# Attention and SwiGLU on one core: V loads behind a cast, wider dummies, block 10 one output later, loads held from chunk 20

## The chip, the cores and the metric

The kernel runs on one core of a Trainium2 chip. The metric is the device time of one execution in microseconds. Each kernel is run several times, and the median of the runs is compared. One more execution is recorded by the hardware profiler; all lines of the profile come from it.

The engines are called PE (matmuls; PEld is its weight load), DVE (vector), ACT (scalar), POOL (GpSimd) and SP (sync). In this kernel POOL issues the loads, SP issues transposing DMAs, and ACT issues the output DMAs. DMAs that POOL issues convert from 32 bits to 16 as they go.

## The reference

q, k and v have 8 batches, 8 heads, 576 positions and 64 features. Causal attention with a window of 64 is followed by a SwiGLU block over 4608 tokens of 512 features:

```
scores = where((0 <= i - j) & (i - j < 64), q @ k.T / 8, -1e9)
x = (softmax(scores) @ v), heads side by side            # 4608 x 512
out = (silu(x @ w_gate) * (x @ w_val)) @ w_out           # 512 -> 1536 -> 512, 32-bit result
```

## The kernel before, in words

**Tiles.** Tokens are cut into 36 chunks of 128; four chunks make one of 9 token groups of 512. For a chunk n, the scores (`S`, lines 454 to 518) are small matmuls of kT and qT; ACT takes the exponential into pt, DVE multiplies with a mask (`m`, line 526). `AV` multiplies pt with v, DVE divides by the sums into xb, and x is transposed into xT, by PE (`X`, line 723) or by a DMA of SP (line 714). From chunk 8 on two chunks are handled together: `P` (lines 1003 to 1014) is the first half of AV for n and n+1, the scores of n+2 and n+3, and the second half. `F` c.f (line 767) is one of 12 column blocks of gate and value for group c: 4 + 4 matmuls of 512 columns, a tanh on ACT and two operations on DVE. `O` c.u (line 804) is the output of 128 tokens: 12 matmuls, an eviction on ACT (line 825) and the output DMA (line 828). `F` of group c needs xT of its four chunks, `O` of group c needs all its `F`.

**Order.** PE's order is written by hand. `build` writes the front: dummy matmuls (`warm`, line 754), the transposes of the first k and q, scores and AV of chunks 0 to 3, the first F of group 0. Then the list `EARLY` (line 180) follows, and from group 3 on `program` (line 1039) gives a regular order: F, F, O, P, F, m. In front of each entry `pump` (line 921) puts out what is ready of two lists: `LOADS` (line 186), which POOL issues, and `SHIPS` (line 194), the transposes that SP issues (Tk14 and Tq14 are those of chunk 14, x8 that of xb of chunk 8). Both are strictly in order. An entry like `k14@O0.1` waits, in its list, until O0.1 is in the program, and carries a semaphore wait for the end of the first PE operation of that entry; on POOL, everything listed behind it waits too. k and q of chunks 0 to 7 come in pairs (k2.2 are chunks 4 and 5) and are transposed on PE (`T2`, line 404).

**Front loads.** `loads` (line 861) puts out, in this order: k of chunks 0 and 1 by SP and ACT (`first_loads`, line 730); q of chunks 0, 1 and k, q of chunks 2, 3 by POOL; constants by DVE and POOL (masks, lines 317 to 335); then on POOL v of chunks 0 to 3, gate and value weights (`load_w`; `W(0, 2)` is both for column blocks 0 and 1), and `shift`: copies of half of a v chunk into the buffer vs, which AV of chunks 1 to 3 reads. `first_T` (line 736) begins with a cast of the loaded k on DVE (line 739; in the profile under line 295) and goes on with the first transposes of PE.

**Waits.** `_Graph.emit` puts a semaphore wait in front of an instruction for each dependence that its engine has not seen yet. `op(..., after=x)` adds one on x. PSUM banks are chosen by a planner's estimate of when they are free.

Of the kernel before, what the change touches and what calls it, by code (L numbers as in the profile page):

```python
# [166 lines left out]
class _Kernel:  # L167
# [12 lines left out]
    EARLY = """  # L180
        V F0.4 F0.5 F0.6 k2t q2t F0.7 S4 F0.8 H4.1.1/act H5.0.1/act B4 F0.9 X4/act+ k3t A5 N5 F0.10 X5/act+ q3t F0.11 S6
        F1.0-1a F1.2-3a B6 F1.4-5a F1.6-7a X6/act+ A7 N7 F1.8-9a X7/act F1.10-11a F1.0-1b F1.2-3b S8 S9 F1.4-5b F1.6-7b
        O0.0 F1.8-9b O0.1 P8 m10 m11 F1.10-11b O0.2 P10 O0.3 X10/act X11/act m12 O1.0 m13 F2.0 F2.1 F2.2 F2.3 F2.4 O1.1
        P12 F2.5 m14 F2.6 m15 F2.7 O1.2 P14 F2.8 m16 F2.9 m17 F2.10 F2.11 O1.3 K O2.0
    """
    LOADS = """
        k2.2 q2.2 Wg8-10 Wv8-10 v4 v5 Wg10-12 Wv10-12 k3.2 q3.2 v6 v7 k8 q8 k9 q9 Wo0-6 k10 q10 k11 q11 Wo6-12 v8 h6.1.0
        h7.0.0 v9 k12 q12 k13 q13 v10 v11 k14@O0.1 q14 k15 q15 v12 v13 k16 q16 k17 q17 v14 k18 q18 v15 k19 q19 q20 v16
        k20 q21 v17 k21 q22 v18 v19 k22@F3.4 q23@F3.4 k23@F3.4 q24@F3.4 v20@F3.4 k24@O2.3 q25@O2.3 v21@F3.4 k25@O2.3
        q26@O2.3 v22@O2.3 k26@O3.1 q27@O3.1 v23@O2.3 k27@O3.1 q28@O3.1 v24@O3.1 k28@O3.3 q29@O3.3 v25@O3.1 k29@O3.3  # L190
        q30@O3.3 v26@O3.3 k30@O4.1 q31@O4.1 v27@O3.3 k31@O4.1 q32@O4.1 v28@O4.1 k32@O4.3 q33@O4.3 v29@O4.1 k33@O4.3
        q34@O4.3 v30@O4.3 k34@O5.1 q35@O5.1 v31@O4.3 k35@O5.1 v32@O5.1 v33@O5.1 v34@O5.3 v35@O5.3
    """
    SHIPS = """
        Tk8 Tq8 Tk9 Tq9 Tk10 Tq10 Tk11 Tq11 Tk12 Tq12 Tk13 Tq13 x8 x9 Tk14 Tq14 Tk15 Tq15 Tk16 Tq16 Tk17 Tq17 x12 x13
# [206 lines left out]
    def T2(self, st, x, engs):  # L402
        g = self.g
        src = (self.ks2 if x == "k" else self.qs2)[st % 2]
        dst = self.kT if x == "k" else self.qT
        z0 = (2 * st) % self.NZ
        for cc in range(2):
            bank, bk = self.bank("a")
            tb = bank[:, 0:256].bitcast(BF).rearrange("p (c j t) -> p c j t", c=2, j=2)

            def pe(e, cc=cc, tb=tb):
                for c in range(2):
                    for j in range(2):
                        for p in range(2):
                            r = e.transpose(tb[64 * p:64 * p + 64, c, j, :], src[:, 4 * cc + 2 * c + p, j, :], self.ident[:, :])  # L415
                return r

            g.op("pe", pe, reads=["ident", ("s2", x, st % 2, 0), ("s2", x, st % 2, 1)], writes=[bk])
            d = dst[:, 2 * cc:2 * cc + 2, 128 * z0:128 * z0 + 256].rearrange("p c (t j) -> p c t j", j=2)
            a = tb.rearrange("p c j t -> p c t j")  # L420
            self.copy(engs[cc], d, a, [bk], [(x + "T", z, cc) for z in (z0, z0 + 1)])
            self.drop([(bank, bk)])
# [282 lines left out]
    def X(self, n, eng="sp", kind="f", half=False):  # L705
        if n >= NCH:
            return
        g = self.g
        ix, it, u = n % 4, (n // 4) % self.NX, n % 4
        xb = self.xb[ix]  # L710
        xo = self.xT[it][:, :, 128 * u:128 * u + 128]
        xk = [("xb", ix, 0), ("xb", ix, 1)]
        if eng == "sp":
            g.op("sp", lambda e: e.dma_start_transpose(xo, xb[:, :]), reads=xk, writes=[("xT", it, u)], dma=True)
            return
        bank, bk = self.bank(kind)
        tb = bank[:, 0:256].bitcast(BF).rearrange("p (c t) -> p c t", c=4)

        def pe(e):
            for c in range(4):  # L720
                for p in range(2 if half else 1):
                    w = 64 if half else 128
                    r = e.transpose(tb[w * p:w * p + w, c, :], xb[:, 128 * c + w * p:128 * c + w * p + w], self.ident[:, :])  # L723
            return r

        g.op("pe", pe, reads=["ident"] + xk, writes=[bk])
        self.copy(eng, xo, tb, [bk], [("xT", it, u)])
        self.drop([(bank, bk)])
# [132 lines left out]
    def loads(self):  # L861
        self.first_loads()
        self.load2(0, "q")
        self.load2(1, "k")
        self.load2(1, "q")
        self.init()
        self.init_ident()
        self.init_mask()
        self.init_nmask()
        for n in range(4):  # L870
            self.load(n, "v")
        self.W(0, 2)
        self.load_w("g", 2, 4)
        self.shift(0, 1, "pool")
        self.shift(1, 1, "pool")
        self.load_w("v", 2, 4)
        self.shift(2, 1, "pool")
        self.shift(3, 0, "pool")
        self.W(4, 6)
        self.W(6, 8)  # L880

# [157 lines left out]
    def program(self):  # L1039
        yield from self.EARLY.split()  # L1040
        for c in range(3, NFC):
            for u in range(4):
                n = 4 * c + u + 4
                yield "F%d.%d" % (c, 3 * u)
                yield "F%d.%d" % (c, 3 * u + 1)
                if c > 3 and (n < NCH or u < 3):
                    yield "O%d.%d" % (c - 1, u)
                elif c == 3 and u != 1:
                    yield "O2.%d" % max(u, 1)
                if n < NCH and u % 2 == 0:  # L1050
                    yield "P%d" % n
                yield "F%d.%d" % (c, 3 * u + 2)
                if n < NCH - 2:
                    yield "m%d" % (n + 2)
                if n >= NCH and u == 3:
                    yield "O%d.%d" % (c - 1, u)
        for u in range(4):
            yield "O%d.%d" % (NFC - 1, u)

    def build(self):  # L1060
        F, S, AV, X, T2, O = self.F, self.S, self.AV, self.X, self.T2, self.O
        self.loads()
        self.banks("a", [4, 5, 6, 7, 0, 1, 2, 3, 4, 5, 0, 1, 2, 3, 4, 5, 6, 7, 0, 1, 2, 3, 4, 5, 6, 7, 6, 7])
        self.warm(48, n=121)
        self.first_T(("dve", "act"))
        s0 = self.Sa(0)
        T2(0, "q", ("act", "dve"))
        self.Sbias(s0)
        self.warm(2)
        self.Sb(s0)  # L1070
        s1 = self.Sa(1, True)
        self.Sb(s1)
        T2(1, "k", ("dve", "act"))
        T2(1, "q", ("dve", "act"))
        self.start()
        s2, s3 = self.Sa(2), self.Sa(3)
        a0, a1, a2, a3 = self.AVa(0), self.AVa(1), self.AVa(2), self.AVa(3)
        self.AVs(a0)
        self.shift(1, 0, "dve")
        self.AVn(a0)  # L1080
        self.shift(2, 0, "dve")
        self.Sbias(s2)
        self.Sb(s2)
        self.AVs(a1)
        self.AVn(a1)
        self.Sbias(s3)
        self.Sb(s3)
        X(0, "dve", "a")
        X(1, "dve", "a")
        self.warm(1, j=2)  # L1090
        self.AVs(a2)
        self.AVn(a2)
        self.AVs(a3)
        self.AVn(a3)
        F(0, (0, 1), 0, 256)
        X(2, "act", "a")
        X(3, "act", "a")
        F(0, (2, 3), 0, 256)
        F(0, (0, 1), 256, 512)
        for n in range(4):  # L1100
            self.did |= {w % n for w in ("s%d", "a%d", "x%d", "Tk%d", "Tq%d")}
        self.main("F0.2-3b")
        self.free = set(range(8))
        self.g.now = dict.fromkeys(self.g.now, max(self.g.now.values()))
        for t in self.program():
            self.pump()
            first = len(self.g.ops)
            self.main(t)
            self.at[t] = next((o for o in self.g.ops[first:] if o.eng == "pe"), None)
        self.pump()  # L1110
        assert not any(self.queues)
        self.g.emit()
# [42 lines left out]
```

## Time and profile before

| | |
|---|---|
| median of 3 runs | 334.22 us (326.64, 334.22, 337.95) |
| profiled execution, its own time | 330.86 us |
| its span, first to last instruction | 329.1 us |
| mean granted clock of PE | 0.995 |
| PE busy | 318.7 us, 97% |
| DVE, ACT, POOL busy | 203.0, 135.8, 108.5 us |
| DMA | 39.85 MB; queue 0 (POOL's loads) 78.4%, queue 1 (transposes) 24.7% of 16 engines |
| landing of v and k loads, median | 6.2 and 5.2 us after issue |
| landing of transposes of k, median (least, most) | 5.7 us (2.5, 10.5) |

Places in the span: the first dummy starts at 1.29 us, the cast at 6.27, the first V load at 5.38, the first F at 17.76. P8 is at about 73, P10 at 78.5, P12 at 97, P14 at 106, F3.0 at 119.4, P16 at 126. From about 130 us on the order repeats every 16.8 us. POOL issues loads until 48.6 us, waits 24.47 us, issues from 73.11 to 97.7, and waits again 34.45 us.

How to read it: a line of the timeline gives start and duration in us, engine, line, operation, result<-inputs, and in brackets the idle time of the engine before it with what ended it. "issue" stands where the profile shows nothing that was waited for. A chain of waits follows the last instruction back to what released it. Landing times of DMAs and the times of single DMA packets are records of the same trace.

### The profile page before, as it was taken

To read this page: it belongs to the slowest core of one execution; us is meant where nothing else is said; L and a number is where in the kernel's file an instruction comes from. 1 tells how busy PE (TensorE), PEld (TensorE's weight loads), DVE (VectorE), ACT (ScalarE), POOL (GpSimd) and SP (SyncE) were. 2 spreads that over 40 slices of the span, in tenths; PEclk is the share of its full clock that TensorE was granted. 3 is DMA by queue.
4 is the path that set the end of the run, shared out by engine and by line. 5 is a ranking of instruction groups with operands and counts; after the bars stand their busy time and mean duration, and the time that the engine had idled before them with its cause. 6 is when DMAs were issued, how large, how long until landed. Compare 5 with 4: busy or idle time off the path is not lost.

```text
span 329.1 us, 8018 instructions
## 1 busy us (share of the span) xinstructions
PE 318.7 (97%) x3415; PEld 171.7 (52%) x3451; DVE 203.0 (62%) x351; ACT 135.8 (41%) x243; POOL 108.5 (33%) x138
## 2 busy tenths in 40 slices
PE   7799999999999999999999999999999999999997
PEld 7475568866455444454545454545454544444443
DVE  4568778738357835866666656565656566555520
ACT  2643865526434544252525252525343432332222
POOL 8899990019960000506060606060512000000000
PEclk9979999999999999999999999999999999999999
DMA  9999999999999999979999999999997111100012
GB/s 144 178 169 181 171 171 138 151 179 140 175 161 152 149 140 166 97 113 117 137 118 124 124 138 112 146 113 131 121 138 94 50 50 48 50 32 33 34 57 102
DMA packets 161571, 39.85 MB, mean 121 GB/s; under 512 B 148608, under 2 KB 157056, under 8 KB 161536
## 3 DMA queue, kind: packets, MB, share of 16 engines
q0 software_dynamic: 111056, 18.62, 78.4%
q1 hardware_dynamic: 45024, 11.22, 24.7%
q10 hardware_dynamic: 5456, 9.51, 9.9%
q8 instruction: 27, 0.44, 0.6%
q14 instruction: 8, 0.07, 0.1%
HBM read 37.75 MB, written 9.44 MB: 143 GB/s over the span
## 4 chain that ended last, share of the span: by engine, by line
PE 92%; issue 2%; DMA 2%; ACT 1%; POOL 1%; DVE 1%; POOLq 0%
PE ps L787 56%; PE ps L818 27%; PE ps L641 3%; DMA va<-in_v_dram 2%; PE ps L505 1%; PE ps L468 1%; PE ps L723 1%; PE ps L843 1%; ACT pt L480 1%; PE ps L592 1%; POOL qs L375 1%; PE ps L472 1%; PE ps L415 0%; PE ps L509 0%; ACT kT L293 0%
## 5 line engine op out<-in xcount | busy, mean ns | idle before, releaser
L795 DVE SCALAR_TENSOR_TENSOR uu<-sig,ps 128x512 bf16<-128x512 bf16 x108 | 73.8, 684 | 63.9 <-ACT sig L793 63.8
L787 PE MATMUL ps<-xT,Wv 128*128 128x512 bf16 (+1 forms) x486 | 111.1, 353 | 0.5
L787 PE MATMUL ps<-xT,Wg 128*128 128x512 bf16 (+1 forms) x479 | 108.8, 353 | 2.6 <-issue 2.4
L793 ACT ACTIVATE sig<-ps 128x512 bf16<-128x512 f32 x108 | 65.0, 602 | 77.2 <-PE ps L787 77.1
L818 PE MATMUL ps<-Wo,hT 128*128 128x512 bf16 x413 | 94.9, 379 | 0.5 <-issue 0.2
L797 DVE SCALAR_TENSOR_TENSOR hT<-uu,ps 128x512 bf16<-128x512 bf16 x108 | 74.1, 686 | 3.9 <-PE ps L787 0.2
L787 PEld LDWEIGHTS ps<-xT,Wv 128*128 128x128 bf16 x496 | 48.9, 99 | 45.3
L366 POOL DMA_DIRECT2D kn<-in_k_dram x31 | 27.9, 902 | 127.9 <-PE ps L818 93.5
L787 PEld LDWEIGHTS ps<-xT,Wg 128*128 128x128 bf16 x496 | 46.7, 98 | 42.8 <-DMA xT<-xb 0.5
L818 PEld LDWEIGHTS ps<-Wo,hT 128*128 128x128 bf16 x420 | 41.0, 98 | 48.5
L825 ACT ACTIVATE ost<-ps 128x512 f32<-128x512 f32 x35 | 20.9, 597 | 90.2 <-PE ps L818 90.2
L366 POOL DMA_DIRECT2D va<-in_v_dram x40 | 35.5, 907 | 12.6 <-PE ps L818 11.9
L366 POOL DMA_DIRECT2D qn<-in_q_dram x31 | 28.1, 915 | 0.0
L668 DVE RECIPROCAL rp<-ps 128x14 f32<-128x14 f32 (+1 forms) x28 | 5.7, 202 | 34.2 <-PE ps L641 34.2
L480 ACT ACTIVATE pt<-ps 128x512 bf16<-128x512 f32 x36 | 18.9, 599 | 7.2 <-PE ps L472 6.4
L517 ACT ACTIVATE pt<-ps 128x512 bf16<-128x512 f32 x36 | 18.6, 603 | 3.7 <-PE ps L509 3.7
L670 DVE TENSOR_TENSOR xb<-ps,rp 128x896 bf16<-128x896 f32 (+1 forms) x28 | 19.4, 692 | 1.0
L641 PEld LDWEIGHTS ps<-va,pt 64*64 64x64 bf16 x888 | 10.9, 107 | 6.1 <-issue 5.1
L641 PE MATMUL ps<-va,pt 64*64 64x65 bf16 x888 | 13.5, 194 | 0.1
L526 DVE TENSOR_TENSOR pt<-pt,kmask 128x1024 bf16<-128x1024 bf16 x18 | 12.3, 684 | 0.0
L526 DVE TENSOR_TENSOR pt<-pt,mask 128x1024 bf16<-128x1024 bf16 x14 | 9.4, 685 | 0.9 <-ACT pt L480 0.9
L472 PE MATMUL ps<-qT,kT 64*64 64x64 bf16 x288 | 7.7, 194 | 1.4 <-issue 1.4
(65 smaller groups left out, 139.8 us busy)
## 6 DMA issues: line engine op xcount, KB each, us to landing
out_dram<-ost ACTq DMA_DIRECT2D x35, 256.0 KB, 2.9
va<-in_v_dram POOLq DMA_DIRECT2D x32, 128.0 KB, 6.2
kn<-in_k_dram POOLq DMA_DIRECT2D x25, 128.0 KB, 5.2
qn<-in_q_dram POOLq DMA_DIRECT2D x25, 128.0 KB, 5.5
Wg<-in_moe_w_gate_dram POOLq DMA_DIRECT2D x6, 256.0 KB, 7.7
Wv<-in_moe_w_val_dram POOLq DMA_DIRECT2D x6, 256.0 KB, 7.7
Wo<-in_moe_w_out_dram POOLq DMA_DIRECT2D x2, 768.0 KB, 19.1
qs<-in_q_dram POOLq DMA_DIRECT2D x3, 256.0 KB, 7.3
```

The source lines that it names most:

```text
L366: self.g.op("pool", lambda e, d=d, a=a: e.dma_start(d, a), writes=ks, dma=True, after=self.hold)
L480: g.op("act", lambda e, po=po, p=p: e.activation(po, sv[p], ACTF.Exp, scale=SCALE), reads=[bx[p][1]], writes=[pk[p]])
L517: g.op("act", lambda e, po=po, p=p: e.activation(po, sv[p], ACTF.Exp, scale=SCALE), reads=[bx[p][1]], writes=[pk[p]])
L526: self.g.op("dve", lambda e: e.tensor_tensor(pt, pt, m, ALU.mult), reads=pk + [key], writes=pk)
L641: z = e.matmul(self.psa[64 * c:64 * c + 64, o:o + 65], pt[p][rows, h, 64 * a:64 * a + 64], va[m][rows, h, 0:65], start=first, stop=phase = ...
L670: g.op("dve", lambda e, d=d, num=num, rb=rb: e.tensor_tensor(d, num, rb, ALU.mult), reads=bk + [("rp", k)], writes=xk, cost=(1.0, 0.25)[k])
L787: r = e.matmul(bank[:, a * n:a * n + n], W[:, kk, f * 128:f * 128 + 128], xT[:, kk, lo:hi], start=(kk == 0), stop=(kk == NK - 1))
L793: g.op("act", lambda e, G=bank: e.activation(sig[:, 0:w], G[:, 0:w], ACTF.Tanh, scale=0.5), reads=[bk], writes=[("sig", i)])
L795: g.op("dve", lambda e: e.scalar_tensor_tensor(uu[:, 0:w], sig[:, 0:w], 1.0, G[:, 0:w], ALU.add, ALU.mult), reads=[("sig", i), gk], writes ...
L797: g.op("dve", lambda e: e.scalar_tensor_tensor(out, v3(uu), 0.5, v3(V), ALU.mult, ALU.mult), reads=[("uu", i), vk], writes=[("hT", ih, f) ...
L818: r = e.matmul(OB[:, :], hT[:, f, 128 * u:128 * u + 128], self.Wo[:, f, :], start=(f == 0), stop=(f == NF - 1), skip_group_check=mid is no ...
L825: g.op("act", lambda e: e.activation(ost[:, :], OB[:, :], ACTF.Copy), reads=[ok], writes=[("ost", io)])
```

## The change

- `loads` ends after the constants. The rest moves into `next_loads`, which `build` calls after `first_T`. The V load of chunk 0 gets a wait for the first DVE operation of `first_T`, the cast; the others stand behind it on POOL.
- Among these the order changes: shift(0, 1) goes from POOL to DVE, behind AVs of chunk 0; shift(1, 1) now stands before the gate weights of blocks 2 and 3, and the value weights of blocks 2 and 3 behind shift(3, 0).
- The dummies are 11 of 512 columns in place of 48 of 121.
- In `EARLY`, P10 comes after O0.3 (it was before it), O1.0 comes before the transposes X10, X11, and O1.1 before F2.0 (it was after F2.4). O2.1 comes before F3.0 (it was after F3.1, out of `program`).
- In `LOADS`, k14 waits for O0.2 and not O0.1; k20, q21, k21, q22, v18, v19, which had no wait of their own, wait for F2.9, and v17 comes ahead of them.

```diff
-        O0.0 F1.8-9b O0.1 P8 m10 m11 F1.10-11b O0.2 P10 O0.3 X10/act X11/act m12 O1.0 m13 F2.0 F2.1 F2.2 F2.3 F2.4 O1.1
-        P12 F2.5 m14 F2.6 m15 F2.7 O1.2 P14 F2.8 m16 F2.9 m17 F2.10 F2.11 O1.3 K O2.0
+        O0.0 F1.8-9b O0.1 P8 m10 m11 F1.10-11b O0.2 O0.3 P10 O1.0 X10/act X11/act m12 O1.1 m13 F2.0 F2.1 F2.2 F2.3 F2.4
+        P12 F2.5 m14 F2.6 m15 F2.7 O1.2 P14 F2.8 m16 F2.9 m17 F2.10 F2.11 O1.3 K O2.0 O2.1
...
-        h7.0.0 v9 k12 q12 k13 q13 v10 v11 k14@O0.1 q14 k15 q15 v12 v13 k16 q16 k17 q17 v14 k18 q18 v15 k19 q19 q20 v16
-        k20 q21 v17 k21 q22 v18 v19 k22@F3.4 q23@F3.4 k23@F3.4 q24@F3.4 v20@F3.4 k24@O2.3 q25@O2.3 v21@F3.4 k25@O2.3
+        h7.0.0 v9 k12 q12 k13 q13 v10 v11 k14@O0.2 q14 k15 q15 v12 v13 k16 q16 k17 q17 v14 k18 q18 v15 k19 q19 q20 v16
+        v17 k20@F2.9 q21@F2.9 k21@F2.9 q22@F2.9 v18@F2.9 k22@F3.4 q23@F3.4 v19@F2.9 k23@F3.4 q24@F3.4 v20@F3.4 k24@O2.3
...
         self.init_nmask()
+
+    def next_loads(self, after):
+        self.hold = after
         for n in range(4):
             self.load(n, "v")
+            self.hold = None
         self.W(0, 2)
+        self.shift(1, 1, "pool")
         self.load_w("g", 2, 4)
-        self.shift(0, 1, "pool")
-        self.shift(1, 1, "pool")
-        self.load_w("v", 2, 4)
         self.shift(2, 1, "pool")
         self.shift(3, 0, "pool")
+        self.load_w("v", 2, 4)
...
-                elif c == 3 and u != 1:
-                    yield "O2.%d" % max(u, 1)
+                elif c == 3 and u > 1:
+                    yield "O2.%d" % u
...
-        self.warm(48, n=121)
+        self.warm(11)
+        first = len(self.g.ops)
         self.first_T(("dve", "act"))
+        self.next_loads(next(o for o in self.g.ops[first:] if o.eng == "dve"))
...
         self.AVs(a0)
+        self.shift(0, 1, "dve")
         self.shift(1, 0, "dve")
```

More of the change, by code (lines that the diff above doesn't have):

```diff
@@ L187 @@
         k2.2 q2.2 Wg8-10 Wv8-10 v4 v5 Wg10-12 Wv10-12 k3.2 q3.2 v6 v7 k8 q8 k9 q9 Wo0-6 k10 q10 k11 q11 Wo6-12 v8 h6.1.0
-        h7.0.0 v9 k12 q12 k13 q13 v10 v11 k14@O0.1 q14 k15 q15 v12 v13 k16 q16 k17 q17 v14 k18 q18 v15 k19 q19 q20 v16
-        k20 q21 v17 k21 q22 v18 v19 k22@F3.4 q23@F3.4 k23@F3.4 q24@F3.4 v20@F3.4 k24@O2.3 q25@O2.3 v21@F3.4 k25@O2.3
-        q26@O2.3 v22@O2.3 k26@O3.1 q27@O3.1 v23@O2.3 k27@O3.1 q28@O3.1 v24@O3.1 k28@O3.3 q29@O3.3 v25@O3.1 k29@O3.3
-        q30@O3.3 v26@O3.3 k30@O4.1 q31@O4.1 v27@O3.3 k31@O4.1 q32@O4.1 v28@O4.1 k32@O4.3 q33@O4.3 v29@O4.1 k33@O4.3
-        q34@O4.3 v30@O4.3 k34@O5.1 q35@O5.1 v31@O4.3 k35@O5.1 v32@O5.1 v33@O5.1 v34@O5.3 v35@O5.3
+        h7.0.0 v9 k12 q12 k13 q13 v10 v11 k14@O0.2 q14 k15 q15 v12 v13 k16 q16 k17 q17 v14 k18 q18 v15 k19 q19 q20 v16
+        v17 k20@F2.9 q21@F2.9 k21@F2.9 q22@F2.9 v18@F2.9 k22@F3.4 q23@F3.4 v19@F2.9 k23@F3.4 q24@F3.4 v20@F3.4 k24@O2.3
+        q25@O2.3 v21@F3.4 k25@O2.3 q26@O2.3 v22@O2.3 k26@O3.1 q27@O3.1 v23@O2.3 k27@O3.1 q28@O3.1 v24@O3.1 k28@O3.3
+        q29@O3.3 v25@O3.1 k29@O3.3 q30@O3.3 v26@O3.3 k30@O4.1 q31@O4.1 v27@O3.3 k31@O4.1 q32@O4.1 v28@O4.1 k32@O4.3
+        q33@O4.3 v29@O4.1 k33@O4.3 q34@O4.3 v30@O4.3 k34@O5.1 q35@O5.1 v31@O4.3 k35@O5.1 v32@O5.1 v33@O5.1 v34@O5.3
+        v35@O5.3
     """
```

## The prediction, on record before the result

> **What bounds the kernel now.** I read the slices of the page first, then the chain of waits, then the waits of PE, and last the timelines of the two stretches that the change edits.
>
> ```profile
> PE   7799999999999999999999999999999999999997
> PEclk9979999999999999999999999999999999999999
> DMA  9999999999999999979999999999997111100012
> ...
> q0 software_dynamic: 111056, 18.62, 78.4%
> ...
> q8 instruction: 27, 0.44, 0.6%
> ```
> PE is full from the third slice on, so only waits of PE move the end. The DMA engines are full until 255 us: whatever PE waits for late comes through them.
>
> ```profile
> 14.19 1.43 issue
> 15.62 0.22 PE ps L472 x2
> ```
> ```profile
> 17.00:18.00 1.00, 0.96 (x30) 0.72 (x23) 0.90 (x3) 0.16 (x1) 1.00 (x2) 0.65 1.27 166
> 18.00:19.00 1.00, 1.00 (x6) 0.71 (x5) 0.95 (x3) 0.00 (x0) 1.00 (x3) 0.50 1.15 140
> ```
> These are the chain of waits from 10 to 20 us, and the table by microsecond (the third number from the right is the granted clock). In the middle of the scores of chunk 3 PE stands 1.41 us with nothing to wait for, and from 17.30 to 20.71 us the clock is 0.5, which costs half of 3.41 us, 1.7 us.
>
> ```profile
> 126.28 0.43 issue
> ```
> ```profile
> 52.03 0.83 PE L787 MATMUL ps<-xT,Wg 128*128 128x256 bf16 x6 [0.19 <-issue]
> ```
> ```profile
> PEld ps L787 <- DMA xT<-xb: 0.5, 1, 0.5
> ```
> The first is the chain of waits at block 16: by the landing records the transpose of q chunk 20 came at 126.62, so this is a DMA wait. The second is a page of instructions (below). The third is F3.0: the transpose of x15 landed at 119.34 and F3.0 began at 119.39; about 0.2 us of it is PE's. All gaps of PE together are 8.0 us.
>
> **How I read the 1.41 us.** Queue q8 carries 27 packets of 16 KB, and PE has 3415 + 3451 instructions and some 90 waits: 256 instructions a packet. PE stopped after 448 instructions of the program; with 64 ahead of the program that is 512, the end of the second packet. On this count the third packet was asked for when PE passed 256 (9.26 us), was served at 13.34, took 0.97 and PE went on at 15.62: 6.4 us. Checked at another place: PE passes 1280 at 45.08, the packet is served at 48.47, and PE, at 1536, starts again at 52.03, the 0.19 us line above. In the full stretches the packet begins 4.94, 4.77 and 4.70 us after the crossing (84.31, 97.35, 106.18 us); with 0.95 of transfer and 1.3 until PE runs, 7.0 us.
> [...]
>
> **The change, part by part.**
> Dummies. 48 narrow ones started 4.81/48 = 0.100 us apart; eleven of 512 columns are 11 x 512/121 x 0.100 = 4.7 us. They end some 0.2 us earlier, and PE then waits for the cast (6.27 to 6.94) as before: 0. But 37 dummies with their weight loads are 74 instructions fewer, so every packet border falls 74 instructions later. I moved each border by 74 in the trace. Border 512 falls in AVs of chunk 2, asked for at 10.52; with 6.4 us it comes at 16.9. Without the old stall PE would be there at about 15.7; it waits 1.2, and F0 starts at 17.8 against 17.76: 0. The border that now passes harmlessly stands at 2816 + 74, inside P12: asked for at 92.3, with 7.0 us there at 99.35, reached at 97.68: **+1.67**. The 0.19 at 52.03 goes, since 47.01 to 54.10 is 7.1 us against 6.6 to 6.9: **-0.19**.
>
> V loads. POOL issued them from 5.38 (0.9 each); behind the cast it is 7.05, 1.67 later. Behind them on POOL stand the W loads and the shifts. Wv 2-4 moves from 12.95 to about 16.05, since shift(3,0) ahead of it waits for V3 (15.36). What hides this is the queue itself: q of chunks 2, 3 lands at 10.54 and V0 at 11.37, V1 12.21; a load on an idle queue needs 2.7 us (132.15 to 134.83), so V0 from 7.05 is ready before its turn. Wv 2-4 issued at 16.05 lands by the row of 15.97 (5.6 us) at 21.6; its matmul starts at 22.26. I take 0; if the cover is gone it is +1.67, and it could be below nothing by what the thinner queue gives to the packet (C). shift(0,1) costs DVE 0.28 to 0.57 in its queue before AVn(0); X0 waits for xb1, 14.69 then 15.0, inside the wait for the packet: 0. POOL loses 0.61.
>
> Block 10 one output later. O0.3 (2.59) now stands before P10, O1.0 and O1.1 around X10, X11. Nothing is added; P10 had no wait (78.5), F2.0 started without one (85.55) and x9 landed at 84.59, so 0; F2.0 gains 2.59 of cover. P12 stays where it was. O2.1 goes ahead of F3.0, which gives x15 2.59 more: **-0.2**.
>
> k14 after O0.2. POOL waits until O0.2 ends (78.55) and not O0.1 (72.80): 5.75 later, and all loads up to v17 stand behind it, and SP's transposes behind those.
>
> ```profile
> 73.11 0.88 POOL L366 DMA_DIRECT2D kn<-in_k_dram  x1 [24.47 <-PE ps L818]
> 73.97 0.88 POOL L366 DMA_DIRECT2D qn<-in_q_dram  x1
> ```
> ```profile
> 75.64 2.55 SPq L714 DMA_TRANSPOSE xT<-xb  x2
> 78.24 1.37 SPq L399 DMA_TRANSPOSE kT<-kn  x1
> 79.65 2.37 SPq L399 DMA_TRANSPOSE qT<-qn  x1
> ```
> The first is POOL's timeline, the second SP's. x8, x9 (75.64) now run ahead of the loads (2.5 us as at 143.41, not 6.7 and 7.7), and leave the crowd. In it transposes land about 2.3 us apart, and 1.0 us alone; two fewer give back 2.0 to 3. So q15's transpose, 93.62 before, comes at 93.62 + 5.75 - 2.3 = 97.1, wanted by the scores of 15 at 97.4: 0. q17's, 105.08, comes at 108.5, wanted at 106.5: 2.0 us, of which the 1.67 in P12 already gives 1.67: **+0.3**. Bounds: -0 (crowd half as deep) and +4.3 (nothing given back).
>
> Loads from chunk 20 behind F2.9 (110.0). k20 left POOL at 89.2 but landed only at 113.12, behind the others; from 110 it lands at about 117, and the transposes of chunks 20 to 22 (until 130.4 now) are wanted by P18 at 140. Queued behind k20 on POOL are q21 to v19 and the loads @F3.4: 10 us of cover, 0. While they are held, the transposes up to q20 meet fewer packets, and PE is 2 us later at P16: **-0.43**.
>
> Sum: 1.67 - 0.19 - 0.2 + 0.3 - 0.43 = +1.15, say 1.2 us. On the profiled execution (330.86: span 329.1 and 1.8 around it) this is 332.0. The four executions known are 326.64, 330.86, 334.22, 337.95, mean 332.4; on the mean it is 333.6, on the median 335.4. I take 332.8, between the first two: +1.2 on a base of 331.6.
>
> **The clock.** A wait of 1.67 us around P12 could bring a second half-clock stretch: 1.7 us, as after 14.21. [...]
>
> **Rivals.**
> A, the forecast: small terms that nearly cancel, 332.8. Chance 0.5.
> B, slower: the held loads. If the crowd gives nothing back, q17's transpose lands at 105.08 + 5.75 = 110.83 and P14 waits 4.3; q20's at 132.4 against 130.6 adds 1.8; less 0.4 for the gaps that go: 331.6 + 5.7 = 337.3, with one more half-clock stretch 339. It decides from the moment q17's transpose lands after 106.5 plus whatever P12 waited. For it: 1.4 us of slack only. Against: x8, x9 leave the crowd. 0.2.
> C, faster: the packets come in time and the front closes up. Without stall and half clock F0 starts at 16.5, is then bound by W (Wv 2-4 at 20.3) and reaches F0.4 at 24.65 and not 26.84: -2.2; with -0.8 for the other gaps: 331.6 - 3.0 = 328.6. For it: fewer loads are queued when the packet is asked for. Against: all measured crossings in full stretches took over 3 us. [...] 0.2.
> D: the V cover is gone, +1.67 on A: 334.5. 0.1. That the V hold and the hold of k20 change nothing is within A: both loads wait in a full queue anyhow.
>
> **Numbers.** 332.8. The range takes in C less the spread of the runs and B with its clock: 327 to 339. 2% (6.7 us, about what a measurement of this kernel can tell from no change, given its spread of 11 us) is 327.5 and 340.9 on the median: faster 0.15 (C, with a base at the low runs), slower 0.1 (half of B), same 0.75.
>
> **What would show it.** POOL's first V load at 7.05 and V0 still landing near 11.4; PE's idle time inside AVs of chunk 2 and not in the scores of chunk 3; an idle stretch of 1 to 2 us inside P12 or ahead of the second scores of P14; no wait at F3.0 and P16; k14 leaving POOL 5.75 us later relative to P8. I am wrong if the front shifts by over 2 us either way, or if P12 and P14 together wait over 4 us.

## The result, and the profile after

The changed kernel takes 333.51 us in the median of 6 runs (330.36 to 334.40); the kernel before 331.38 us (326.64 to 337.95, 6 runs, the three known before among them). The ratio is 1.014 [1.010, 1.018]; in a second session, with 12 runs of the changed kernel, it was 1.008 [1.004, 1.012]. All ratios here compare fast runs alone: runs more than 1.5% above the fastest of their kernel are left out. The change makes the kernel slower by about 1%, which is less than the 2% that I took as the least that one measurement can tell; I had forecast +1.2 us on a base of 331.6, so 332.8. The profiled execution takes 333.54 us, its span 331.8.

The 40 slices and the queue of POOL's loads, from the page of the changed kernel:

```profile
PE   6789998999989899999999999999999999999997
...
PEclk9999999999999999999999999999999999999999
DMA  9999999999999993999999898989896211100012
...
q0 software_dynamic: 111056, 18.62, 76.0%
```
The front looks better than before (clock full from the first slice on), but PE has dips at slices 3, 7, 12 and 14: 17 to 25, 50 to 58, 91 to 100 and 108 to 116 us. The waits of PE in the changed kernel (in all, times, longest):

```profile
PE ps L593 <- issue: 1.6, 1, 1.6
...
PE ps L469 <- DMA qT<-qn: 1.3, 1, 1.3
PE ps L788 <- DMA Wv<-in_moe_w_val_dram: 1.2, 1, 1.2
PE ps L724 <- DVE xb L612: 1.2, 1, 1.2
PE ps L469 <- issue: 1.0, 1, 1.0
```
Line numbers are one to six higher than in the kernel before. In order of time: X0 waits for xb of chunk 0 (14.51), F0 for the value weights of blocks 2 and 3 (Wv 2-4 below; 20.13), the AV of chunk 7 has nothing to wait for (53.07, first line), the second scores of P12 wait for the transpose of q15 (98.03), those of P14 for that of q17 (108.56, last line; its transpose landed at 109.51). All gaps of PE add up to 13.1 us, against 8.0.

The same places of both profiled executions, by the operation that follows (us):

| place | before | after | difference |
|---|---|---|---|
| tanh of F0.0 | 19.69 | 17.97 | -1.71 |
| tanh of F0.2, behind the wait for Wv | 24.20 | 23.32 | -0.89 |
| tanh of F1.4-5a, the third of F1 | 50.78 | 49.89 | -0.89 |
| tanh of F1.8-9a, the fifth of F1, behind the wait at 53.07 | 55.34 | 55.86 | +0.52 |
| division in P8 | 73.84 | 74.37 | +0.53 |
| division in P12 | 98.10 | 100.07 | +1.98 |
| division in P14 | 107.20 | 110.44 | +3.24 |
| division in P16 | 127.47 | 129.88 | +2.41 |
| division in P18 | 141.61 | 144.21 | +2.60 |

So the front gains 1.7, and then loses it and 2.6 more, in four steps: F0, the wait at 53 us, P12, P14. P16, which had a wait before, gives 0.8 back. From P18 on the difference stays within 0.1.

The gain: the table by microsecond of the changed kernel, with the granted clock third from the right, where it was 0.5 before, and no wait in the scores of chunk 3.

```profile
17.00:18.00 1.00, 1.00 (x11) 0.89 (x10) 0.96 (x3) 0.03 (x1) 1.00 (x2) 1.00 1.17 146
```
Where it goes first: the chain of waits of the changed kernel, 7 to 26 us (start, duration, what).

```profile
7.02 1.77 POOL va L367 x2
8.79 5.72 DMA va<-in_v_dram
14.51 0.05 issue
14.56 0.73 POOL vs L296
15.34 0.56 POOL vs L296
15.90 5.42 DMA Wv<-in_moe_w_val_dram
21.31 0.04 issue
21.36 4.54 PE ps L788 x40
```
Before, the chain left a V load (that of chunk 1) at 12.21 and was PE's from 12.68 on:

```profile
6.29 5.93 DMA va<-in_v_dram
...
12.68 0.22 PE ps L468
```
Now it runs from the held V loads through V2, the two shifts and the issue of Wv 2-4 to F0: the V part is on the path until 21.3.

Where it goes later: POOL's timeline at k14, SP's behind it, and the chain from O0.2 to P12, all of the changed kernel.

```profile
79.35 0.88 POOL L367 DMA_DIRECT2D kn<-in_k_dram  x1 [29.62 <-PE ps L819]
```
```profile
76.17 2.51 SPq L715 DMA_TRANSPOSE xT<-xb  x2
83.41 2.84 SPq L400 DMA_TRANSPOSE kT<-kn  x1
86.98 1.26 SPq L400 DMA_TRANSPOSE qT<-qn  x1
88.34 1.66 SPq L400 DMA_TRANSPOSE kT<-kn  x1
90.04 1.39 SPq L400 DMA_TRANSPOSE qT<-qn  x1
```
```profile
76.50 2.55 PE ps L819 x11
79.05 0.30 issue
79.35 0.88 POOL kn L367
80.23 0.85 POOL qn L367
81.08 7.25 DMA kn<-in_k_dram
...
90.04 9.16 DMA qT<-qn
99.20 0.09 issue
```
PE releases k14 with the end of O0.2 (79.05), and 20 us later it waits for what it released: two loads are issued, k15's takes 7.25 us to land, the transposes of k14, q14 and k15 go ahead on SP, and q15's lands 9.16 us after its issue.

### The profile page after: what moved, and what is told of

Same layout as the page of the kernel before. It is cut to its first block, busy times and chain, and to the rows that moved or that the text cites. A ratio compares the mean times of both kernels' runs of the same rounds, so it can differ in the third digit from the quotient of the medians.

```text
span 331.8 us, 7934 instructions
## 1 busy us (share of the span) xinstructions
PE 316.2 (95%) x3379; PEld 167.5 (50%) x3414; DVE 202.9 (61%) x352; ACT 136.2 (41%) x243; POOL 107.9 (33%) x137
## 4 chain that ended last, share of the span: by engine, by line
PE 83%; DMA 8%; POOL 3%; issue 2%; DVE 1%; ACT 1%; SPq 0%; POOLq 0%
PE ps L788 52%; PE ps L819 25%; DMA qT<-qn 3%; PE ps L642 2%; DMA kn<-in_k_dram 2%; DMA va<-in_v_dram 2%; DMA Wv<-in_moe_w_val_dram 2%; PE ps L506 1%; PE ps L844 1%; PE ps L469 1%; POOL va L367 1%; POOL qs L376 1%; SPq L400 0%; POOL vs L296 0%; PE ps L416 0%
## 5 line engine op out<-in xcount | busy, mean ns | idle before, releaser
L481 ACT ACTIVATE pt<-ps 128x512 bf16<-128x512 f32 x36 | 19.1, 597 | 6.9 <-PE ps L473 6.0
L469 PE MATMUL ps<-qT,kT 64*64 64x128 bf16 x144 | 7.3, 219 | 2.7 <-DMA qT<-qn 1.3
## 6 DMA issues: line engine op xcount, KB each, us to landing
Wo<-in_moe_w_out_dram POOLq DMA_DIRECT2D x2, 768.0 KB, 19.9
```

The source lines that it names most:

```text
L481: g.op("act", lambda e, po=po, p=p: e.activation(po, sv[p], ACTF.Exp, scale=SCALE), reads=[bx[p][1]], writes=[pk[p]])
```

## The experiments

Three causes could make the 2.6 us and the swallowed 1.7: the k14 hold with its chain to P12 and P14 (my 0.3 mis-sized), the late V loads (the cover gone), and the packets of instructions, moved by the wide dummies. Sixteen runs came in four groups, two of them repeats; in the names, a_ is one edit on the changed kernel, b_ one part alone on the kernel before. The differences are near 1 us while runs of the kernel before spread over 14 us, and the granted clock of an execution says why (last section). So beside each ratio (95%) stands the mean of the executions whose granted clock was 1.0 (0.999 counted with it), with standard error and number; the kernel before has 328.10 +- 0.10 there (82 of its 134 executions in the four sessions).

| kernel | ratio to before | mean at clock 1.0 | P10 / P12 / P14 waits in the profile |
|---|---|---|---|
| changed, both sessions | 1.014, 1.008 | 332.08 +- 0.32 (15) | 0 / 1.3 to 1.4 / 1.0 to 1.8 |
| a_k14early | 1.005 [1.002, 1.009] | 330.00 +- 0.22 (10) | 0 / 0.15 / 0.6 |
| a_vold | 1.004 [1.001, 1.008] | 330.24 +- 0.35 (9) | 0 / 2.2 / 0 |
| a_narrow | 1.005 [1.001, 1.009] | 330.33 +- 0.47 (7) | 0 / 1.6 / 0.7 |
| a_wv | 1.009 [1.005, 1.012] | 331.57 +- 0.45 (9) | 0 / 2.6 / 0 |
| a_k14late | 1.018 [1.012, 1.024] | 333.00 +- 0.93 (2) | 0 / 3.3 / 0 |
| a_vold_k14early | 0.999 [0.996, 1.003] | 328.60 +- 0.29 (12) | 0 / 0.4 / 0 |
| b_wide | 1.000 [0.997, 1.003] | 328.88 +- 0.17 (10) | 0 / 0 / 0.6 |
| b_vnew | 1.005 [1.000, 1.010] | 330.04 +- 0.43 (7) | 0.6 / 0 / 0.4 |
| b_vhold | 1.003 [0.998, 1.008] | 329.66 +- 0.49 (7) | 3.0 / 0 / 0.3 |
| b_worder | 1.002 [0.997, 1.006] | 328.45 +- 0.39 (6) | 0 / 0 / 0 |
| b_order_lists, run twice | 0.998, 0.998 | 328.48 +- 0.24 (22) | 0 / 0.5 to 1.4 / 0 to 0.5 |
| b_order_k20 | 1.000 [0.996, 1.003] | 328.73 +- 0.21 (10) | 0 / 0 / 0.9 |
| b_m22 | 1.003 [1.000, 1.007] | 328.87 +- 0.38 (7) | 2.6 / 0 / 0 |
| b_m22_order_k20 | 1.001 [0.997, 1.005] | 328.56 +- 0.33 (12) | 0 / 0 / 1.7 |

A mean at clock 1.0 leaves out executions with a half-clock stretch, which in the profiles came behind waits of 1.41 to 3.3 us, so it can understate a price; the ratios with their wide intervals say the same order. At clock 1.0 the changed kernel costs 4.0 +- 0.3 us. The same choice also leaves out what the kernel before loses by its half-clock stretches, which it has more often (52 of 134 executions, the changed kernel 3 of 18). Over all executions the means are 332.6 +- 0.4 (18) and 330.05 +- 0.26 (134): there the change costs 2.5 +- 0.5 us. The prices below are prices at clock 1.0. Each profile is of one execution, and not always of one at clock 1.0; where it isn't, the text says so.

### First group: one part undone, and the dummies alone

**a_k14early**, the changed kernel with k14 released by O0.1:

```diff
-        ... v10 v11 k14@O0.2 q14 ...
+        ... v10 v11 k14@O0.1 q14 ...
```


> The changed kernel with k14 waiting for O0.1 again and not O0.2; all else as changed. Hold theory (the later loads of chunks 14 to 17 make the transposes of q15 and q17 late): the waits before the scores in P12 (1.27 us) and P14 (1.04 us) go, F2.0 doesn't wait since O1.1 now stands ahead of it; 2.2 to 2.8 us less than the changed kernel, 331 us. Order theory (the waits come from block 10 standing one output later): they stay, and the time with them. Queue theory (V loads): they stay.

Measured: 330.00 at clock 1.0, 2.1 +- 0.4 less than the changed kernel. The wait for the transpose in P12 is gone and that in P14 is 0.6. Two of its waits of PE:

```profile
PE ps L788 <- DMA Wv<-in_moe_w_val_dram: 1.0, 1, 1.0
...
PE ps L469 <- issue: 0.6, 1, 0.6
```
What follows: the k14 hold costs 2 us, half of the change. The first line stays, so F0's wait is not of this hold. There was no wait near 53 us, though the packet borders stand where they do in the changed kernel: the packet was served 1.9 us after PE crossed the border, and not 5.6.

**a_vold**, the changed kernel with the V part undone (V loads, copies and weights in the old place and order):

```diff
-    def next_loads(self, after):
-        self.hold = after
...
-        self.next_loads(next(o for o in self.g.ops[first:] if o.eng == "dve"))
...
-        self.shift(0, 1, "dve")
```


> The changed kernel with the V loads, the weight loads and the copies of V issued as before. Queue theory: all three later waits (AV of chunk 7, P12, P14) shrink by over half, and the time falls by 3 us or more, to 330 us. My theory: only the wait for the value weights of blocks 2 and 3 (1.23 us at 20.1 us) goes; F0 gains at most 1.2 us, less where the front is in the half clock; P12 and P14 still wait about 1 us each; time 0 to 1.5 us less than the changed kernel.

Measured: 330.24, 1.8 +- 0.5 less than the changed kernel. The wait for Wv is gone; P12 waits longer:

```profile
PE ps L469 <- DMA qT<-qn: 2.2, 1, 2.2
```
What follows: the V part costs about as much as the k14 hold; 1.8 lies between the two expectations. The profiled execution is one with a half-clock stretch (clock 0.995, from 99.21 on) and does not show where the 1.8 us are won: in it PE comes to P12 sooner, waits longer, and its division in P12 stands at 100.02, against 100.07 in the changed kernel.

**b_wide**, the kernel before with the dummies of the changed one:

```diff
-        self.warm(48, n=121)
+        self.warm(11)
```


> The kernel before with the 11 wide dummies alone. Border theory (74 PE instructions fewer move the borders of the instruction packets): the 1.4 us wait in the scores of chunk 3 goes to AV of chunk 2 or vanishes, and a new wait of 0.5 to 1.6 us stands in the AV of chunk 7, near 54 us; in the median about +1 us (0 to +1.6). Queue theory (the later V loads push all DMAs back, and the wait near 53 us is one for data): no wait over 0.3 us near 54 us, and a time within 0.5 us of before, or 1.4 us less.

Measured: 328.88, +0.8 +- 0.2; the ratio shows no difference. The profile has no wait in the scores of chunk 3, none at 53 us beyond 0.2, and 0.6 in P14. Against the profiled execution of before, P8 comes 3.2 us earlier and the span is 3.3 shorter; against the kernel's mean at clock 1.0 nothing is gained. What follows: the half-clock stretch in the profiled execution of the kernel before is not in most of its executions. 82 of 134 executions of the kernel before have no half-clock stretch at all, so most had nothing of this to give. The wait that the border theory expected near 54 us did not come.

**a_narrow**, the changed kernel with the old dummies:

```diff
-        self.warm(11)
+        self.warm(48, n=121)
```


> The changed kernel with the 48 narrow dummies again. Border theory: the 1.56 us wait in the AV of chunk 7 (53.07 us) goes, and a wait in the scores of chunk 3 near 14 us comes back, which the wait for value weights of blocks 2 and 3 (21.3 us) covers in part: 1.0 to 1.5 us less than the changed kernel, 332 us. Queue theory: the wait near 53 us stays at 1 us or more, and the time is that of the changed kernel (333.5 us).

Measured: 330.33, 1.75 +- 0.55 less than the changed kernel. No wait at 53 us, and none in the scores of chunk 3, where one was expected; PE waits 1.5 for a copy of V at 12.90, has a half-clock stretch from 16.65 to 20.07 (clock 0.995), and then P12 waits 1.6 and P14 0.7. What follows: inside the change the wide dummies may cost more than alone (1.75 against 0.8; the difference, 0.95 +- 0.6, is not clear of the noise). 5 of the 12 executions had a half-clock stretch; over all executions the gain is 0.9 +- 0.75.

### Second group: the parts alone, and a repeat

**after_again** is the changed kernel once more.

> The changed kernel itself, unedited, beside the others on one chip. Sum of what the profiles of the first four show: V part 1.7 us in the front where it isn't under a half clock, hold of k14 2.1 us: ratio 1.008 to 1.014, fast runs near 331. If the wait in AV of chunk 7 (1.56 us) belongs to the change and not to that one execution, it is there again and the ratio is 1.014 or more; if it is chance, it is under 0.5 us here.

Measured: 331.85 +- 0.31 (10 executions); its waits of PE:

```profile
PE ps L469 <- issue: 1.8, 1, 1.8
PE ps L469 <- DMA qT<-qn: 1.4, 1, 1.4
```
What follows: the waits in P14 and P12 come again; the one at 53 us is absent from this execution, so it is no fixed part of the change, and the time is the same without it. 

**b_vnew**, the whole V part (hold, order, shift on DVE) on the kernel before; its diff is that of a_vold read the other way.

> The kernel before with the V part alone: V loads behind the cast, the copies and the weight loads in their new order; narrow dummies, order and lists as before. Weights theory: the value weights of blocks 2 and 3, issued some 3 us later, land at 20.5 to 21.5 us and not 20.3; where PE runs at full clock it waits 0.5 to 1.3 us for them, and P8 comes 1 to 1.7 us later than in the wide-dummies run; +0.5 to +1.7 us in the fast runs, and no wait in P12 above 0.3 us. Cover theory (mine on record: a full queue hides it): within 0.3 us of before.

Measured: 330.04, +1.9 +- 0.4; PE waits 1.4 for Wv, 0.6 in P10 and 0.4 in P14. What follows: with a_vold (1.8), the V part's price is about 1.9 in both surroundings.

**b_order_lists**, the new order and both holds (k14, k20) on the kernel before:

```diff
-        O0.0 F1.8-9b O0.1 P8 m10 m11 F1.10-11b O0.2 P10 O0.3 X10/act X11/act m12 O1.0 m13 F2.0 F2.1 F2.2 F2.3 F2.4 O1.1
+        O0.0 F1.8-9b O0.1 P8 m10 m11 F1.10-11b O0.2 O0.3 P10 O1.0 X10/act X11/act m12 O1.1 m13 F2.0 F2.1 F2.2 F2.3 F2.4
...
-        ... k14@O0.1 ... k20 q21 ...
+        ... k14@O0.2 ... k20@F2.9 q21@F2.9 ...
```


> The kernel before with the new order of block 10 and both holds (k14 at O0.2, k20 at F2.9); V part and dummies as before. Hold theory: waits of 1 to 2.2 us together ahead of the scores in P12 and P14, +1.5 to +2.2 us. Front theory (those waits need the front's later queue): under 0.5 us together, and the time of before.

Measured: 328.46, +0.4 +- 0.4, no difference. P12 and P14 wait only 0.5 each. This I did not understand: the same hold that costs 2 us in the changed kernel costs nothing here, although its chain from k14 to q15's transpose is as long (19.1 us).

**a_wv**, the changed kernel with Wv of blocks 2 and 3 ahead of shift(2, 1) and shift(3, 0):

```diff
+        self.load_w("v", 2, 4)
         self.shift(2, 1, "pool")
         self.shift(3, 0, "pool")
-        self.load_w("v", 2, 4)
```


> The changed kernel with the value weights of blocks 2 and 3 issued ahead of the copies shift(2,1) and shift(3,0), as before; V loads still behind the cast. Weights theory: their wait at 20.1 us (1.23 and 0.95 us in two profiles) goes or falls below 0.3; 0.8 to 1.5 us less than the changed kernel at full clock. If the V loads themselves are what is late (V2 landed 14.51 and not 13.04), the front gains under 0.5 us, since X0 and AV of chunks 2, 3 then set it.

Measured: 331.57, 0.5 +- 0.55 less than the changed kernel. Two of its waits of PE:

```profile
PE ps L469 <- DMA qT<-qn: 2.6, 1, 2.6
...
PE ps L788 <- DMA Wv<-in_moe_w_val_dram: 0.5, 2, 0.2
```
What follows: the wait for Wv falls from 1.2 to twice 0.2, and P12 takes the gain back with a wait of 2.6, in an execution with a half-clock stretch from 98.76 on (clock 0.995). Over the executions at clock 1.0 the gain is not clear of the noise either.

### Third group: the hold pushed further, and the border theory by itself

**a_k14late**, the changed kernel with k14 released by O0.3 (2.6 us later):

```diff
-        ... k14@O0.2 ...
+        ... k14@O0.3 ...
```


> The changed kernel with k14 waiting for O0.3, one output later still. Hold theory: from k14's issue to the landing of q15's transpose it takes 19 to 21 us in every profile so far, and P12's second scores come 18.5 us after O0.2 ends; with O0.3 only 15.9 are left, so PE waits 3.5 to 5 us in P12 and the runs without a half-clock stretch come 2 to 3 us above the changed kernel (334 to 335). If the waits come from the order or from the front, the time stays at 332.

Measured: ratio 1.018; 333.00 in the two executions at clock 1.0 (the other four had a half-clock stretch). P12's wait:

```profile
PE ps L469 <- DMA qT<-qn: 3.3, 1, 3.3
```
The profile is of an execution with a half-clock stretch, as in two of three here. What follows: 2.0 us more of wait in P12 for 2.6 us of delay, while P14's wait goes. The wait of 3.3 is a little under the 3.5 to 5 us expected, and the time at clock 1.0, 0.9 +- 1.0 above the changed kernel, settles nothing; over all executions it is 1.6 +- 0.65 above (334.2 +- 0.5). The chain from k14's issue to q15's transpose takes 19.3 us, as in the other kernels; it moves with the hold and does not shorten.

**b_m22**, the kernel before with dummies of another size, 26 fewer, so that the packet borders stand elsewhere:

```diff
-        self.warm(48, n=121)
+        self.warm(22, n=256)
```


> The kernel before with 22 dummies of 256 columns: as many columns as the 11 wide ones, 52 PE instructions fewer than before, 22 more than with 11. Border theory: the border of the second packet falls behind the scores of chunk 3 (no 1.4 us wait there), and that of the sixth before AV of chunk 7, so a packet has 7.8 us and not 6.7: no wait over 0.3 us in either place, and runs without a half-clock stretch 0.3 to 1.2 us under before (328.05). If the width of the dummies itself costs (wide dummies alone: +0.8), the time is that of the wide ones, 328.9.

Measured: 328.87, +0.8 +- 0.4. No wait for a packet anywhere in the profile, and P8 3.3 us earlier than in the profiled execution of before; then P10 waits 2.6 for its transposes (the releaser printed is the last that ended before):

```profile
PE ps L468 <- DVE xb L670: 2.6, 1, 2.6
```
What follows: the theory that packets set the time falls; 0.3 to 1.2 us less had been expected. Taken away, they leave an earlier front and, in this execution, a wait about as long where PE next needs the load stream; with that wait and the half-clock stretch behind it, P12 comes 0.7 us later than before.

**b_order_k20**, b_order_lists with k14 left at O0.1:

```diff
-        ... k14@O0.2 ...
+        ... k14@O0.1 ...
```


> The kernel before with the new order of block 10 and the hold of chunk 20 alone; k14 waits for O0.1, V part and dummies as before. Hold theory: no wait over 0.3 us in P12, none at F3.0 and P16: 0 to 0.6 us under before. If the order is what makes P12 and P14 wait, 1 us or more above it.

Measured: 328.73, +0.6 +- 0.2; no wait at P10 and P12, 0.9 in P14. What follows: order and k20 hold together gain nothing, where up to 0.6 had been expected, and beside b_order_lists (328.48) the k14 hold is free here (-0.25 +- 0.3).

**b_m22_order_k20** joins the last two, the parts that had looked harmless.

> The parts that the theories call free or good together: 22 dummies of 256 columns, the new order, the hold of chunk 20; k14 at O0.1 and V part as before. Border and hold theories: 0.5 to 1.8 us under before in runs without a half-clock stretch, 326.3 to 327.5. If the gains of the front are taken back by later DMA waits, within 0.3 us of before.

Measured: 328.56, +0.5 +- 0.35; P14 waits 1.7. At clock 1.0 no combination that was run beats the kernel before.

### Fourth group: what in the V part costs, and when the k14 hold costs

**b_vhold**, the V loads held behind the cast on the kernel before, the order of copies and weights as it was:

```diff
+    def next_loads(self, after):
+        self.hold = after
         for n in range(4):
             self.load(n, "v")
+            self.hold = None
...
+        self.next_loads(next(o for o in self.g.ops[first:] if o.eng == "dve"))
```


> The kernel before with the V loads behind the cast alone; copies and weight loads in their old order. Stream theory (POOL's loads up to 73 us are one stream that never catches up, so time lost at its head stays): value weights of blocks 0 and 1 land at 17.3 to 17.8 us and not 15.7 to 16.8, the whole stream is 0.8 to 1.2 us late, and runs without a half-clock stretch come 0.7 to 1.5 us above before. Cover theory (mine on record): within 0.3 us of before.

Measured: 329.66, +1.6 +- 0.5. The first wait of PE, and the chain of waits at P10:

```profile
PE ps L468 <- DMA qT<-qn: 3.0, 1, 3.0
```
```profile
72.61 7.67 DMA qT<-qn
80.28 0.09 issue
80.37 0.22 PE ps L468 x2
```
What follows: POOL's start, 1.65 us later at 7 us, is not made up by the stream of loads. k13's load, one of its last before POOL waits, landed at 66.3 to 70.5 us in the ten executions with the old V part (mean 67.8), and at 69.8 to 73.8 in the six with the new one or the hold alone in which it is known (mean 71.1). At P10 it shows as a late transpose of q13. Here the transpose also met more: it was issued 1.3 us later than in the kernel before (72.61 against 71.29) and took 7.67 us in place of 2.83, while POOL had begun to load k14 at 70.89, ahead of it, and before only at 73.11. That these loads slowed it is argued, not shown. The transpose itself landed at 71.6 to 75.2 in the executions with the old V part (two of them at 78.0 and 78.6), at 76.9 to 81.2 in those with the new one or the hold alone.

**b_worder**, only the new order of copies and weights, with shift(0, 1) on DVE, no hold:

```diff
         self.W(0, 2)
-        self.load_w("g", 2, 4)
-        self.shift(0, 1, "pool")
         self.shift(1, 1, "pool")
-        self.load_w("v", 2, 4)
+        self.load_w("g", 2, 4)
         self.shift(2, 1, "pool")
         self.shift(3, 0, "pool")
+        self.load_w("v", 2, 4)
```


> The kernel before with the copies and weight loads in the new order alone (one copy on DVE); V loads at their old time. Stream theory: V lands as before, the value weights of blocks 2 and 3 land 0.5 to 1.2 us later than with the old order, the stream behind them is as much late, runs without a half-clock stretch 0.4 to 1.2 us above before. If only the V hold counts: within 0.3 us of before.

Measured: 328.45, +0.35 +- 0.4, and a wait of 1.35 for Wv. What follows: the wait for Wv in the front is mostly of the order, but the time at clock 1.0 is of the hold. 6 of the 12 executions had a half-clock stretch.

**b_order_lists_2** is b_order_lists again.

> The run with the new order and both holds and the front of before, once more. If the first result (+0.4 us, interval with zero) was right: -0.3 to +0.8 us, and P12 and P14 together wait 0 to 1.1 us in the profile. If it was chance and the hold costs the same everywhere: +1.5 to +2.2 us.

Measured: 328.50 +- 0.30; two of its waits of PE, in the scores of chunk 3 and in P12:

```profile
PE ps L473 <- issue: 1.4, 1, 1.4
PE ps L469 <- DVE hT L798: 1.4, 1, 1.4
```
What follows: the hold being free with narrow dummies and old V loads is no accident of one session, even though this execution had a wait of 1.4 in P12, more than the 0 to 1.1 expected; q15's transpose had landed at 96.93, just before that wait ended.

**a_vold_k14early**, the changed kernel with V part and k14 hold both undone (wide dummies, order and k20 hold remain; the diffs are those of a_vold and a_k14early).

> The changed kernel with the V part as before and k14 at O0.1: wide dummies, new order, hold of chunk 20. With the old V part and the hold it took 330.24 in runs without a half-clock stretch. Hold theory: the price of the hold is 1.5 to 2 us here too, so 328.2 to 328.8. If the hold costs only together with the late V part: 330 again.

Measured: 328.60, +0.5 +- 0.3; P12 waits 0.4, for ACT. What follows: without these two parts nothing is left of the 4 us. Against a_vold the k14 hold costs 1.6 +- 0.45 here too.

### The sum of the prices

At clock 1.0: V part 1.8 to 1.9, of which 1.6 the hold; k14 hold 1.6 to 2.1 with the wide dummies, about nothing with narrow dummies and old V; wide dummies +0.8 alone; order and k20 hold +0.6 alone. They don't simply add: alone the three parts make 0.8 + 1.9 + 0.4 = 3.1 us, together 4.0, a difference that is not clear of the noise; and wide dummies, order and k20 hold together make 0.5 (a_vold_k14early), not 1.4.

Open: why the k14 hold is free beside narrow dummies. The chain is as long there (19.1, 20.0 us), and PE's waits in P12 (0.5, 1.4) lie only partly below those of the others (1.3 to 2.6). It seems to go with the dummies and not with V: with the new V part and narrow dummies (a_narrow against b_vnew) order and both holds add only 0.3 +- 0.65. One reading, argued only: with narrow dummies PE loses time in the front anyway, so that it reaches O0.2 and P12 with the stream ahead of it. No run tells this apart from an effect of the packets' places.

Open too: the five runs with the new order and the old V part that leave out the k14 hold or the wide dummies or both (b_order_lists twice, b_order_k20, b_m22_order_k20, a_vold_k14early) had a half-clock stretch in only 4 of 60 executions, where the kernel before had one in 52 of 134. Over all executions their mean is 328.9 +- 0.2 us, 1.1 +- 0.35 under that of the kernel before, though at clock 1.0 they gain nothing. No run was made to find what in them does it.

## Why the prediction was wrong

The forecast was "same" by small terms that nearly cancel. The range held 333.51, but the change is a slowdown of 4.0 +- 0.3 us at full clock, over three times my +1.15 (2.5 +- 0.5 over all executions). Two terms were mis-sized, and both are the same mistake: a delay of POOL's load stream priced as if the stream had slack.

- **k14 after O0.2, +0.3: measured 2.0 +- 0.4.** This is the step that failed. I let the transposes of x8 and x9, which leave the crowd, "give back 2.0 to 3", and so put q15's transpose at 97.1 against a need at 97.4. x8 and x9 did leave the crowd, as I said: they landed at 78.75 and 79.88, 2.5 us after issue. But the rest did not become quicker: from k14's issue to q15's landing it took 19.9 us in the changed kernel, and 19.1 to 21.4 in all the others with the hold at O0.2; before it was 20.5 (73.11 to 93.62), so 0.7 us came back and not 2.3. From k14's issue to the second scores of P12 PE has 18.7 us of other work (79.35 to 98.03), so 1.2 us is missing, and q15's landed at 99.20. That is rival B's "nothing given back", 93.62 + 5.75 = 99.4. B's sum, 337.3, was too high: it charged 4.3 at P14, where P12 and P14 together waited 2.3, and 1.8 for q20's transpose at P16, which landed at 123.91 and cost nothing. The price of 2.0 is that of this hold inside this change; beside narrow dummies it was about nothing, for a reason that stays open.
- **V loads, 0: measured 1.8 to 1.9.** What was to hide it was "the queue itself", because the DMA engines were full. V0 and Wv 2-4 did land where I said (10.62 against 11.4; 21.31 against 21.6); V2 landed late (14.51, against 13.04 before), V3 did not (14.81, against 15.36). But landing in time for the front is not the test. The time lost at the head of the stream was still missing at its end, where k13's load landed 3.3 us later in the mean. In b_vhold it was waited for at P10; that it goes into P12 and P14 where the k14 hold stands is argued, not shown. Rival D had the size, +1.67, and I gave it 0.1. With the page's DMA row at 9 or 7 until 255 us, which I showed myself, it should have had the higher chance.
- **Dummies in the front, 0: -1.7, and worth nothing.** I counted 6.4 us for the packet at border 512, due at 16.9. It was served 2.1 us after the crossing and landed at 13.32, 3.0 us before PE needed it. So the front closed up as rival C said, stall and half clock gone. But C priced against the one execution that had them; at clock 1.0 the kernel before takes 328.1, which is C's 328.6 without any change. And what PE gained in front it waited for at P10 or P12 in the profiles of b_m22 and a_wv.
- **Packet border in P12, +1.67: nothing there.** That packet landed at 94.69, 5 us before its first instruction was due. My 4.7 to 4.9 us from the crossing to the packet were three rows of one execution, and what I held against rival C, that all crossings in full stretches took over 3 us, was not so in that same profile: by the same count border 512 was crossed at 15.62 and its packet served at 17.77, border 768 at 25.75 and at 27.82. In the changed kernel it is 1.2 to 5.6 us at the crossings before 110 us, and nothing at one of them. Where I forecast 1.67 + 0.3 = 1.97 us of wait in P12 and P14 and 2.3 came, the agreement is luck: the cause was the transposes, not the packet. The place was wrong; a packet did cost 1.56 us in this execution, but at 53.07, where I had predicted a gain of 0.19:

```profile
54.63 0.22 PE L593 MATMUL ps<-va,pt 128*64 128x65 bf16 x1 [1.56 <-issue]
```
The count (256 instructions a packet, 64 ahead of the program) is my estimate; PE's stops at 15.62 and 52.03 before and at 54.63 here fall on it. By the same count it was asked for at 46.22; it was served at 51.84 and landed at 53.07. The other execution of the same kernel (after_again) has no such wait. The packet wait came in one of two executions, and my count could not tell in which.
- **Block 10 one output later, 0, and O2.1 ahead of F3.0, -0.2; k20 hold, -0.43: the waits as forecast, the sum not.** F3.0 has no wait, P16 waits 0.35 for ACT and no more for a transpose, and gives back 0.8 us. But alone the two make +0.6 +- 0.2 and not -0.6 (b_order_k20); in its profile PE waits 0.9 at P14, which I had not counted.
- **The clock.** A further half-clock stretch behind a wait near P12 stood in my upper bound. The profiled execution has none; a_vold shows one from 99.21 to 102.62, behind its wait of 2.2.
- **The base.** 332.8 came near 333.5 because the base, 331.6, held a half-clock stretch that the kernel before has in a part of its executions. Against 328.1, its time at full clock, the same sum would have given 329.3, and the changed kernel takes 332.1.

By the test I had set: the front shifted by 1.7 us (the bound was 2), and P12 and P14 together waited 2.3 (the bound was 4). Both bounds were too wide to catch an error of 2.8 us (4.0 against 1.15).

## What to carry to other kernels

Here the DMA engines were nearly full until 255 us, and a delay of 1.65 us at the head of POOL's loads cost 1.6 +- 0.5 (b_vhold). Where one queue is as full, price a delay at its head, until a run shows otherwise, at its full length at the next place where the busy engine needs that queue, whatever lands "in time" nearby. A hold on a load is priced by the whole chain that it starts, measured from release to the last landing (here 20 us against a budget of 18.7), not by what the removed traffic might give back. And when two things run neck and neck, PE and a load stream here, a gain of one can come back as a wait for the other (in b_m22 P8 came 3.3 us earlier, and then P10 waited 2.6): test a gain in the front by the next meeting place, not by the front. And a mean over executions chosen by their clock answers another question than a mean over all: here 4.0 us against 2.5.

## What the runs showed of the hardware

- **Most of the spread of one kernel goes with the clock.** The kernel before ran 134 times in these sessions, from 326.6 to 340.3 us. Sorted by the mean granted clock of each execution they fall into groups: at 1.0, 328.10 +- 0.10 us (82 executions); at 0.995, which in every profile with that clock is one half-clock stretch of 3.41 us, 331.41 +- 0.19 (30); at 0.99, by the same count two stretches, 334.60 +- 0.27 (17); at 0.985, three, 338.46 +- 0.47 (5). No execution with two or three was profiled. Each stretch goes with 3.2 to 3.9 us, not with the 1.7 that half speed for 3.41 us makes when worked out. The other half is perhaps the wait that brings the stretch; this is argued, not shown.
- **Half-clock stretches came behind waits of 1.41 us and more, but the length of the wait did not decide.** They began behind waits of 1.41 us (the kernel before), 1.5 (a_narrow), 2.2 (a_vold), 2.6 (b_m22, a_wv) and 3.3 (a_k14late). Waits of 1.3 and 1.6 in the changed kernel brought none, nor did 1.4 in b_order_lists_2, in the same scores as the 1.41, nor 3.0 in b_vhold. What decides is not shown. The changed kernel had a stretch in 3 of 18 executions, the kernel before in 52 of 134.
- **A transpose by DMA took 2.5 us or 9.2 in one execution, the profiled one of the changed kernel.** x8 and x9, ahead of the held loads, landed 2.5 us after issue; q15's took 9.16, behind the transposes of k14, q14 and k15 and while POOL's loads were landing.
